# A list-scheduled attention and MLP kernel, planned with longer durations and longer hand-overs

## The chip, the cores and the metric
The kernel runs on one core of a Trainium2 chip. The metric is the device time of one execution in microseconds (us). The engines are called as in the profile: PE is TensorE (PEld its weight loads), DVE is VectorE, ACT is ScalarE, POOL is GpSimd, SP is SyncE, which issues the DMAs.

## The reference
Three stages follow one another. The attention keeps only scores near the row's maximum; the middle stage is a LayerNorm and a two-layer MLP with a residual; the last rotates by cosine and sine of a product, mixes tokens and channels, and adds.

```python
# attention: B=4, H=8, S=576, D=64
scores = q @ k.T / sqrt(64)
scores = where(scores >= max(scores) - tau, scores, -1e9)
x = softmax(scores) @ v                # -> [4, 576, 512]
# MLP
xn = (x - mean) / sqrt(var + 1e-6) * g
x = x + relu(xn @ w1) @ w2             # 512 -> 2048 -> 512
# mixing
theta = x @ w_theta
zr, zi = x * cos(theta), x * sin(theta)
y = w_tok_r @ zr + w_tok_i @ zi        # over the 576 tokens
u = x + y
out = u + relu(u @ w_ch)
```

## The kernel before
All work is written as a list of operations, and a planner orders it. `op` (class Plan, L288) records a function that emits one or a few instructions, the operations that it depends on, the buffers ("slots") that it takes and frees, a key, and for each engine that may run it a planned duration in ns (T for PE, V, A and G for DVE, ACT and POOL, Q for SP's DMAs). `run` (L319) plays the list several times in a planned time: `play` (L371) gives each engine its next ready operation, an operation with several possible engines goes to the one that would be done first by the plan, and after a dependency on another engine LAT ns pass before the user may start (`hop`, L366), after a DMA also DMA_LAT. `latest` (L345) works out from a played order how late each operation could start; these ranks, averaged over the plays, decide between ready operations on DVE, ACT, POOL and SP. PE takes the ready operation with the smallest key. Only the last play emits instructions, each engine's in the order of the plan. On the chip, instructions wait for semaphores; the planned time is not part of the program.

Planned durations are the numbers written at each `op` call, replaced by those in the table DUR where the operation's name and number stand there; DUR holds the mean durations of a profile.

Where the plan leaves PE idle for more than IDLE = 200 ns until the end of attention, `keep` (L620) writes filler matmuls (L626, 128x256, with a weight load each) into PE's order, as many as fill 0.7 of what is above 200 ns at 110 ns each:

```python
if e == "T" and self.idle and s - before > IDLE:
    self.idle(int((s - before - IDLE) * BUSY / 110.0), before)
```

Attention goes by batch b, tile t of 128 queries and head pair hp (`couple`, L1071): S_b_t_hp is the product of queries and keys (L1101). Batches 0 and 1 use f32 for it, 2 and 3 f16 halves in three products. There are two S buffers in PSUM (NS = 2), and a couple takes both. For each head (`unit`, L1197) DVE computes the row maximum ("top", L1208), ACT masks (L1224) and exponentiates (L1250), the weights are split into a high and a low f16 half (L465 to L478: copies on ACT, DVE or POOL, subtraction L478 on DVE or POOL), transposed by PE (tm, tl; L1179) or by DMA (L1271), and multiplied with v (pv_b_t_hp, L1116 to L1129). Buffers E (4) and P16 (4) hold scores and halves on the way. v is scaled first: pvs_b_hp (L990) sums a maximum, DVE turns it into a scale (L993), ACT applies it (va, L983 to L1008).

The batches are worked in pairs: 9 tiles of a pair form three groups; when a group's attention is done, `ln_group` (L1331) normalizes it, splits it and transposes it by DMA (L1405) into ringX, and `mlp1` (L873) runs the MLP for it: p_A, p_B (L883) and chA, c (L906); p1_A1_1_0 is the first product of the second pair's second group. Weights are read, scaled and split on the way (`cvt`, L634); pw_w2_8 (L781) sums a maximum for the scale of one part of w2, after ACT's L775. MLP matmuls and attention share PE from 106 us on; attention ends at about 417 us. Then come theta (L1883), z (`make_z`, L1941), y (`mix`, L2023, with L2074 and L2080) and o (`chan`, L2089, with L2105 and L2138).

## Time and profile before
| | us |
|---|---|
| median of 3 runs | 805.35 (805.19 to 805.42) |
| the profiled execution | 806.75 |
| its span | 805.0 |
| its mean granted clock | 0.998 |
| attention of batch 0 and the start of batch 1, without MLP matmuls | to 106.1 |
| attention beside the MLP, about | 106.1 to 417 |
| MLP and theta, z, y, o | the rest |

The span is what the profiler saw between the first and the last instruction; the profiled execution's own time has 1.75 us around it. Busy time is counted per engine, and engines run beside one another, so shares add up to more than 100%. A row of a timeline joins instructions of one kind that follow one another without a gap ("x8"). "idle before <-releaser" is how long the engine stood and what ended it. PEclk is the TensorE clock that was granted, as a share of full speed.

### The profile page before, as it was taken

The numbers are of one execution on the slowest core, as the hardware profiler recorded it, in microseconds if no ns is written. First come the engines' busy times: TensorE is split into PE (matmuls) and PEld (weight loads), VectorE is DVE, ScalarE is ACT, GpSimd is POOL, SyncE is SP. The second block draws the span as 40 slices with busy tenths as digits, with TensorE's granted clock in tenths as the row PEclk, the third lists the DMA queues.
The fourth block names the chain that finished last, engine by engine and source line by source line (L and its number), as shares of the span: only waits on it lengthen the run. The fifth ranks groups of instructions, "written<-read, shape, count | busy, mean of one in ns | idle before, by whom it ended". The sixth has DMA issues, their size and how long they took to land.

```text
span 805.0 us, 16588 instructions
## 1 busy us (share of the span) xinstructions
PE 789.7 (98%) x6189; PEld 516.8 (64%) x6189; DVE 650.4 (81%) x1310; ACT 510.0 (63%) x934; POOL 464.2 (58%) x551
## 2 busy tenths in 40 slices
PE   8999899999999999999999999999999999999998
PEld 6877766655566676666655555555545777567776
DVE  4999899999789897989867688777678795689843
ACT  5988899896797887898734243343476361474502
POOL 2767889878767676677436366635136370364711
PEclk9999999999999999999999999999999999999999
DMA  8565799987498998899894533663564005010011
GB/s 229 148 164 152 203 192 185 191 169 183 103 176 156 177 176 180 176 179 177 145 234 103 173 97 110 232 217 130 131 136 140 27 18 108 2 45 16 1 61 59
DMA packets 210833, 110.63 MB, mean 137 GB/s; under 512 B 173120, under 2 KB 191936, under 8 KB 210752
## 3 DMA queue, kind: packets, MB, share of 16 engines
q1 hardware_dynamic: 209936, 109.31, 57.8%
q8 instruction: 48, 0.79, 0.4%
q10 hardware_dynamic: 816, 0.26, 0.1%
q14 instruction: 33, 0.27, 0.1%
HBM read 52.50 MB, written 15.73 MB: 85 GB/s over the span
## 4 chain that ended last, share of the span: by engine, by line
PE 87%; DVE 6%; issue 2%; POOL 2%; ACT 1%; DMA 1%; SPq 0%; DVEq 0%; POOLq 0%
PE p_A L883 16%; PE chA L906 16%; PE y L2047 13%; PE S L1101 9%; PE p_B L883 6%; PE c L906 6%; PE th L1883 5%; PE o L2105 5%; PE pv L1129 4%; PE pv L1116 3%; PE pv L1124 3%; DVE ringE L1208 1%; PE tm L1179 1%; DMA raw_w<-in_w 1%; DVE w L706 1%
## 5 line engine op out<-in xcount | busy, mean ns | idle before, releaser
L883 PEld LDWEIGHTS <-w 128*128 128x128 f16 x1152 | 109.4, 98 | 79.7 <-issue 5.4
L906 PE MATMUL chA<-w,hbuf 128*128 128x512 f16 x648 | 149.9, 379 | 0.2 <-POOL w L478 0.2
L883 PE MATMUL p_A<-ringX,w 128*128 128x384 f16 x864 | 149.1, 326 | 0.0
L906 PEld LDWEIGHTS <-hbuf 128*128 128x128 f16 x864 | 80.8, 98 | 94.0 <-issue 5.8
L1208 DVE TENSOR_SCALAR_CACHE_REDUCE ringE<-S,ncoef 128x576 f32<-128x576 f32 x144 | 113.1, 809 | 14.5 <-PE S L1101 8.5
L478 POOL TENSOR_TENSOR ringP<-ringE,ringP 128x128 f16<-128x128 f32 (+2 forms) x109 | 102.0, 944 | 26.1 <-ACT ringP L465 17.4
L1224 ACT ACTIVATE ringE<-ringE,tiny 128x576 f32<-128x576 f32 x144 | 105.4, 768 | 9.3 <-POOL tiny L1216 4.9
L2047 PE MATMUL y<-tok,z 128*128 128x288 f16 x768 | 97.0, 286 | 0.0
L2047 PEld LDWEIGHTS <-z 128*128 128x128 f16 x768 | 75.1, 98 | 19.3
L1250 ACT ACTIVATE ringE<-ringE,ntaup 128x576 f32<-128x576 f32 x117 | 85.1, 764 | 0.0
L889 ACT ACTIVATE hbuf<-p_A 128x384 f16<-128x384 f32 x72 | 35.1, 488 | 49.8 <-PE p_A L883 46.8
L478 DVE TENSOR_TENSOR ringP<-ringE,ringP 128x512 f16<-128x512 f32 (+2 forms) x73 | 58.5, 813 | 2.4 <-ACT ringP L465 1.3
L1101 PE MATMUL S<-kf,qf 64*128 64x288 f32 (+1 forms) x288 | 53.4, 436 | 1.4 <-DVE ringE L1208 1.4
L469 POOL TENSOR_SCALAR ringP<-ringE 128x576 f16<-128x576 f32 x53 | 38.6, 731 | 23.7 <-ACT ringE L1250 19.6
L883 PE MATMUL p_B<-ringX,w 128*128 128x384 f16 x288 | 50.7, 326 | 0.0
L906 PE MATMUL c<-w,hbuf 128*128 128x512 f16 x216 | 50.6, 379 | 0.0
L1469 DVE SCALAR_TENSOR_TENSOR x<-chA,qs,x 128x512 f32<-128x512 f32 x54 | 40.2, 744 | 12.4 <-PE chA L906 12.1
L892 DVE SCALAR_TENSOR_TENSOR hbuf<-p_A,hbuf 128x384 f16<-128x384 f32 x72 | 39.7, 552 | 12.7 <-ACT hbuf L889 12.3
L2105 PE MATMUL o<-x1T,cw 128*128 128x288 f16 x360 | 44.9, 286 | 1.2 <-DVE x1T L2080 1.2
L473 ACT ACTIVATE x1T<-u,cs 128x576 f16<-128x576 f32 x15 | 11.6, 771 | 50.7 <-DVE u L2074 50.6
L1883 PE MATMUL th<-th,x1T 128*128 128x512 f16 x192 | 42.4, 379 | 0.0
L2105 PEld LDWEIGHTS <-cw 128*128 128x128 f16 x360 | 35.2, 98 | 10.4 <-issue 1.4
(267 smaller groups left out, 1578.0 us busy)
## 6 DMA issues: line engine op xcount, KB each, us to landing
raw_w<-in_w SPq DMA_DIRECT2D x20, 512.0 KB, 4.9
rawe<-in_w SPq DMA_DIRECT2D x12, 512.0 KB, 4.6
raw_tok<-in_wtok SPq DMA_DIRECT2D x12, 432.0 KB, 3.9
xscr<-x SPq DMA_DIRECT2D x18, 256.0 KB, 2.5
xl<-xscr SPq DMA_DIRECT2D x18, 256.0 KB, 4.9
out<-uo SPq DMA_DIRECT2D x15, 288.0 KB, 2.1
vraw<-in_v SPq DMA_DIRECT2D x13, 320.0 KB, 3.8
scr<-ringX SPq DMA_DIRECT2D x5, 768.0 KB, 4.6
```

Source lines behind the costliest of these rows:

```text
L478: e.tensor_tensor(out=out, in0=a, in1=b, op=ALU.subtract)
L883: T.matmul(st["ps"][:, :n], lhsT=ch.w1(a, c), rhs=xt()[:, c, bb, :n], start=(kk == 0), stop=(kk == 11))
L892: V.scalar_tensor_tensor(out=st["h"][:, 1, :n], in0=st["ps"][:, :n], scalar=0.0, in1=st["h"][:, 0, :n], op0=ALU.max, op1=ALU.subtract)
L906: T.matmul(ps, lhsT=h[:, a, t * 128:(t + 1) * 128], rhs=ch.w2(bb), start=(first and (a, bb) == M2[0]), stop=(stop and (a, bb) == M2[2]))
L1101: T.matmul(w["S"][:, n, 0:288], lhsT=qd.q[a][r, hp], rhs=d.k[c][r, n * 288:(n + 1) * 288], start=(k == 0), stop=(k == len(seq) - 1))
L1208: V.tensor_scalar(out=st["e"].rearrange("p (a k) -> p a k", a=2), in0=st["S"][:, :, 0:288], scalar1=ncoef, scalar2=None, op0=ALU.mult, op1 ...
L1224: A.activation(out=st["e"], in_=st["e"], func=AF.Prelu, bias=cp["thr"][:, j:j + 1], scale=-1.0, alpha=STEEP)
L1250: A.activation(out=e_of(ws), in_=e_of(ws), func=AF.Exp, bias=ntaup, scale=1.0)
L1469: V.scalar_tensor_tensor(out=x[p, t0 + t], in0=st["ch", t], scalar=chunks[i].quad.inv, in1=x[p, t0 + t], op0=ALU.mult, op1=ALU.add)
L1883: T.matmul(st["ps"], lhsT=src(a, c), rhs=w[:, c * 512:(c + 1) * 512], start=(kk == 0), stop=(kk == 11))
L2047: T.matmul(st["ps"][n][:, 0:288], lhsT=a, rhs=w[:, n * 288:(n + 1) * 288], start=(k == 0 and q == 0), stop=(k == 8 and q == 2))
L2105: T.matmul(st["ps"][n][:, 0:288], lhsT=w[:, cs], rhs=d["t"][a][:, kk, n * 288:(n + 1) * 288], start=(kk == 0 and q == 0), stop=(kk == 3 an ...
```

## The change
The table DUR and the lookup in `op` are taken out, so planned durations are the written ones: longer for most operations (a top is planned with 830 ns, not 764; a subtraction on DVE with 930, not 783; a step of S with 1230, not 1172), shorter for a few (a guard of the LayerNorm's scale 600, not 1274; chan.fin 457, not 675). LAT goes from 160 to 300 ns, DMA_LAT from 2500 to 2600. `run` no longer plays three times and emits the third; it plays 8 times, keeps the ranks with which the planned span was shortest, and emits a ninth play with those.

```diff
-LAT = 160.0
+LAT = 300.0
...
-DMA_LAT = 2500.0
+DMA_LAT = 2600.0
...
-PICK = 2
-DUR = {
-    "T": {
...
-        "couple.qk.go": {850: 896, 1000: 972, 1020: 990, 1230: 1172},
...
-        "unit.lo16.go": {930: 783},
...
-        "unit.top": {830: 764},
...
-        name = fn.__qualname__.replace("tile_kernel.<locals>.", "").replace("<locals>.", "")
-        engs = {e: DUR.get(e, {}).get(name, {}).get(round(ns), ns) for e, ns in engs.items()}
...
-    def run(self):
+    def run(self, passes=8):
...
-        rank = None
-        for k in range(PICK + 1):
+        best = rank = None
+        for k in range(passes + 1):
...
-            span = self.play(k == PICK)
+            if k == passes:
+                for o, r in zip(self.ops, best[1]):
+                    o.rank = r
+            span = self.play(k == passes)
+            if k == passes:
+                break
+            if best is None or span < best[0]:
+                best = span, [o.rank for o in self.ops]
             late = self.latest(span)
             rank = late if k == 0 else [0.5 * (a + b) for a, b in zip(rank, late)]
```

The program that comes out computes the same with the same instructions, but for three things: their order on each engine, the engine of some (of the 512-wide subtractions L478 118 stand on POOL, 100 before; 59 on DVE, 74 before), and the fillers: 92 instead of 44, 81 instead of 40 of them ahead of the first MLP matmul. Lines of the new kernel are 159 lower (S is L942, a top L1049, pv L957, a filler L467, the scale's L993 now L834).

Three places of the new order follow. In the names the last number is that of the buffer's allocation, which differs between the two.

The first is PE at the first change of the query tile in batch 0, from S_0_1_0 (the second tile's first head pair) to S_0_1_1. Before:

```order
L1101 MATMUL S_0_1_0_1_348<-kf_0_0_120,qf_0_1_228 128x288
L1116 MATMUL pv_0_0_2_360<-vraw_0_2_244,PT_0_0_2_0_329 128x65 x4
L1116 MATMUL pv_0_0_2_360<-vraw_0_2_244,ringP_88 128x65
L1116 MATMUL pv_0_0_2_360<-vraw_0_2_244,PT_0_0_2_1_354 128x65 x4
L1116 MATMUL pv_0_0_2_360<-vraw_0_2_244,ringP_88 128x65
L1101 MATMUL S_0_1_1_0_383<-kf_0_1_147,qf_0_1_228 128x288
```

and after (warm is a filler):

```order
L957 MATMUL pv_0_0_2_344<-vraw_0_2_225,ringP_88 128x65
L957 MATMUL pv_0_0_2_344<-vraw_0_2_225,PT_0_0_2_1_338 128x65 x4
L957 MATMUL pv_0_0_2_344<-vraw_0_2_225,ringP_88 128x65
L942 MATMUL S_0_1_0_0_367<-kf_0_0_120,qf_0_1_267 128x288
L942 MATMUL S_0_1_0_1_368<-kf_0_0_120,qf_0_1_267 128x288
L942 MATMUL S_0_1_0_0_367<-kf_0_0_120,qf_0_1_267 128x288
L942 MATMUL S_0_1_0_1_368<-kf_0_0_120,qf_0_1_267 128x288
L467 LDWEIGHTS one16_92
L467 MATMUL warm_24901_386<-one16_92 128x256
```

What moved: pv_0_0_2 stood between the two steps of S; now it stands ahead of the first, and behind that come 14 fillers (the last two rows are the first of them) and then S_0_1_1. S_0_2_0 and S_0_3_0 are followed by 16 fillers each.

The second is DVE at the start of batch 1, where the scale of v (pvs_1_0, L993 before, L834 after) is computed. Before:

```order
L1208 TENSOR_SCALAR ringE_87,tiny_89<-S_1_4_0_0_1142,ncoef_95 128x576
L706 SCALAR_TENSOR_TENSOR w1_4_1169<-raw_w1_4_1_700,qs_4_113,w1_4_1169 128x512
L467 COPY x_0_4_1194<-pv_0_4_0_1151 64x130
L706 SCALAR_TENSOR_TENSOR w1_4_1169<-raw_w1_4_0_623,qs_4_113,w1_4_1169 128x512
L706 SCALAR_TENSOR_TENSOR w1_4_1169<-raw_w1_4_2_793,qs_4_113,w1_4_1169 128x512
L993 TENSOR_SCALAR tiny_89<-pvs_1_0_1204 128x1
L706 SCALAR_TENSOR_TENSOR w1_4_1169<-raw_w1_4_3_857,qs_4_113,w1_4_1169 128x512
```

and after:

```order
L1049 TENSOR_SCALAR ringE_87,tiny_89<-S_1_4_0_0_1207,ncoef_95 128x576
L834 TENSOR_SCALAR tiny_89<-pvs_1_0_1217 128x1
L604 TENSOR_SCALAR tiny_89<-qs_4_113 128x4
L523 TENSOR_SCALAR a_w2_4_2_1172<-a_w2_4_2_1172 128x512
L1049 TENSOR_SCALAR ringE_87,tiny_89<-S_1_4_1_0_1219,ncoef_95 128x576
L608 SCALAR_TENSOR_TENSOR qs_4_113<-qs_4_113,tiny_89 128x4
```

The scale's operation stood behind three weight operations of 128x512 and a copy that follow the top of S_1_4_0; it now stands right behind that top.

The third is PE where the maximum of a weight part is summed (pw_w2_8), among the MLP's first products of the first pair (p1_A0_0_11). Before:

```order
L883 LDWEIGHTS w1_8_2606
L883 MATMUL p1_A0_0_11_2765<-ringX_80,w1_8_2606 128x384
L883 LDWEIGHTS w1_8_2606
L883 MATMUL p1_A0_0_11_2765<-ringX_80,w1_8_2606 128x384
L781 LDWEIGHTS one16_92
L781 MATMUL pw_w2_8_2773<-tiny_89,one16_92 128x1
L883 LDWEIGHTS w1_8_2606
L883 MATMUL p1_A0_0_11_2765<-ringX_80,w1_8_2606 128x384
```

and after:

```order
L942 MATMUL S_2_0_0_1_2821<-khi_2_0_2785,qhi_2_0_2648 128x288
L942 MATMUL S_2_0_0_0_2820<-khi_2_0_2785,qhi_2_0_2648 128x288
L942 MATMUL S_2_0_0_1_2821<-khi_2_0_2785,qhi_2_0_2648 128x288
L724 LDWEIGHTS w1_8_2603
L724 MATMUL p1_A0_0_11_2805<-ringX_80,w1_8_2603 128x384
L724 LDWEIGHTS w1_8_2603
L724 MATMUL p1_A0_0_11_2805<-ringX_80,w1_8_2603 128x384
L724 LDWEIGHTS w1_8_2603
L724 MATMUL p1_A0_0_11_2805<-ringX_80,w1_8_2603 128x384
L622 LDWEIGHTS one16_92
L622 MATMUL pw_w2_8_2844<-tiny_89,one16_92 128x1
```

The sum stands behind the third matmul of p1_A0_0_11 in both, but the whole step S_2_0_0 (12 matmuls, of which the last three are the first rows here) is now ahead of it.

## Rows read from the trace of the kernel before

**Rows 1.** The page's first part: busy time, share of the span, instructions.
```profile
PE 789.7 (98%) x6189; PEld 516.8 (64%) x6189; DVE 650.4 (81%) x1310; ACT 510.0 (63%) x934; POOL 464.2 (58%) x551
```

**Rows 2.** Busy time by stage: window, length, PE, PEld, DVE, ACT, POOL, clock, DMA share, GB/s.
```profile
6.00:106.10 100.10, 93.40 (x830) 75.88 (x829) 89.25 (x217) 85.41 (x168) 69.80 (x88) 0.98 0.68 180
106.10:404.00 297.90, 295.36 (x2754) 187.35 (x2752) 267.46 (x586) 249.04 (x440) 217.98 (x268) 1.00 0.88 170
```

**Rows 3.** PE's waits: for what, us in total, times, the longest.
```profile
PE pvs L990 <- ACT va L983: 2.9, 3, 1.9
PE pv L1124 <- DVE tiny L993: 1.8, 1, 1.8
PE pw_w L781 <- ACT tiny L775: 1.7, 1, 1.7
...
PE o L2105 <- DVE x1T L2080: 1.2, 1, 1.2
```

**Rows 4.** PE's timeline at 253 to 256 us: start, length, what.
```profile
253.29 0.78 PE L1101 MATMUL S<-khi,qlo 64*128 64x288 f32 x4
...
254.53 0.82 PE L906 MATMUL chA<-w,hbuf 128*128 128x512 f16 x3
255.19 0.60 PE L626 MATMUL warm<-one 128*128 128x256 bf16 x4
255.62 2.11 PE L883 MATMUL p_A<-ringX,w 128*128 128x384 f16 x12
```

**Rows 5.** PE's timeline, start of batch 0.
```profile
9.60 1.03 PE L626 MATMUL warm<-one 128*128 128x256 bf16 x8
...
13.69 1.97 PE L1101 MATMUL S<-kf,qf 64*128 64x288 f32 x8 [0.32 <-DVE ringE L1208]
```

**Rows 6.** DVE's timeline, the same stretch.
```profile
12.47 0.43 DVE L662 TENSOR_SCALAR a_w<-raw_w 128x512 uint32<-128x512 uint32 x1 [1.63 <-DMA raw_w<-in_w]
12.81 0.81 DVE L1208 TENSOR_SCALAR_CACHE_REDUCE ringE<-S,ncoef 128x576 f32<-128x576 f32 x1
```

**Rows 7.** PE's timeline at the first change of the query tile.
```profile
23.66 1.24 PE L1101 MATMUL S<-kf,qf 64*128 64x288 f32 x8
24.83 1.10 PE L1116 MATMUL pv<-vraw,PT 128*128 128x65 f32 x8
```

**Rows 8.** DVE's timeline, the second top of the same S.
```profile
25.68 0.81 DVE L1208 TENSOR_SCALAR_CACHE_REDUCE ringE<-S,ncoef 128x576 f32<-128x576 f32 x1
```

**Rows 9.** PE's timeline, behind the change to the third tile.
```profile
49.40 1.97 PE L1101 MATMUL S<-kf,qf 64*128 64x288 f32 x8 [0.70 <-DVE ringE L1208]
```

**Rows 10.** PE's timeline at 92 us; the window 90 to 100, columns as in rows 2.
```profile
92.41 1.69 PE L1124 MATMUL pv<-va,PT 128*128 128x65 f16 x28 [1.76 <-DVE tiny L993]
...
90.00:100.00 10.00, 8.24 (x74) 6.77 (x74) 7.24 (x17) 7.18 (x14) 8.55 (x13) 0.83 0.60 172
```

**Rows 11.** The LayerNorm of group (0,2): last pv, DMA transposes from 240 to 256 us.
```profile
222.78 1.01 PE L1124 MATMUL pv<-va,PT 128*128 128x65 f16 x28
...
L1405 SPq DMA_TRANSPOSE ringX<-xn x3: 1232/1296/1300, 244.0 to 250.4; - x3
...
DMA to landing us min/median/max: 3.0/3.3/3.3
```

**Rows 12.** PE's timeline ahead of the wait for x1T at 655 us.
```profile
648.13 7.02 PE L2105 MATMUL o<-x1T,cw 128*128 128x288 f16 x56
```

**Rows 13.** Groups by form: the 512-wide subtractions on POOL and on DVE.
```profile
L478 POOL TENSOR_TENSOR ringP<-ringE,ringP 128x512 f16<-128x512 f32 x59 | 71.8, 1220 | 14.2 <-ACT ringP L465 10.7 <-DVE ringP L467 0.9 <-DMA PT<-ringP 0.8
...
L478 DVE TENSOR_TENSOR ringP<-ringE,ringP 128x512 f16<-128x512 f32 x58 | 48.3, 841 | 2.3 <-ACT ringP L465 1.3 <-POOL ringP L469 0.8
```

**Rows 14.** DVE's timeline, then POOL's, around 649 us.
```profile
649.07 0.74 DVE L1970 SCALAR_TENSOR_TENSOR r<-xl,cs,r 128x512 f32<-128x512 f32 x1
649.72 1.77 DVE L1970 SCALAR_TENSOR_TENSOR co<-xl,cs,co 128x512 f32<-128x512 f32 x1
...
649.29 1.65 POOL L2074 TENSOR_TENSOR u<-u,x1T 128x576 f32<-128x576 f32 x1 [1.04 <-DVE u L2069]
```

158 lines of the change are left out of this document (removed).

## The prediction
> **What bounds the kernel now.** I read the page's first part, then the table of stages, then TensorE's waits, then timelines at the places that the order moves. TensorE is busy 98% of the span, the next engine, VectorE, 81% [rows 1]. The first two stages [rows 2], without the first six us: from 6.0 to 106.1 us (attention of batch 0 and the start of batch 1, before the first matmul of the MLP) TensorE is busy 93.40 of 100.1 us; from 106.1 to 404, beside the MLP, it misses 2.5 us of 297.9. So 6.7 of the 9.2 us that TensorE leaves open in the two lie in the first, and there its busy time holds fillers besides (the keep-warm matmuls of L626, 44 in all, 40 of them before the MLP). No order can win much more than the sum of these. The waits [rows 3] name the largest: on ScalarE's va (three, the longest 1.9 us), on VectorE's L993 (1.8), on ScalarE's L775 (1.7), on VectorE's x1T (1.2).
>
> The profiled execution took 806.75 us, a span of 805.0 and 1.75 around it; the median of the runs is 805.35, 1.40 lower. I sum differences against the profiled execution and carry them over to the median.
>
> **The change, part by part.** No arithmetic changes. What changes is the plan that decides order and engines, and how many fillers it writes: 44 before, 92 after. A filler costs 0.108 us: four of them begin at 255.19 and the next matmul at 255.62 [rows 4].
>
> *Start, a gain.* Before, 8 fillers stand behind pvs_0_3, from 9.60 on, and only then S_0_0_1; VectorE then starts on a weight (12.47, after 1.63 us of idling) ahead of that S's top, which so begins at 12.81, and the third S waits until 13.69 [rows 5, 6]. The new order has S_0_0_1 right behind pvs_0_3, and VectorE has both tops ahead of the weight. The 8 × 0.108 = 0.9 us of fillers go, and the top comes ahead of the weight (0.3 us); together that could be 1.2 us at the third S, or nothing if q and v land late. I take **−1.0** (0 to −1.2).
>
> *Tile boundaries of batch 0, a loss.* At S_0_1_0 the old order keeps pv_0_0_2 between this S and the next; the new one puts it ahead of S_0_1_0 and leaves only 14 fillers between S_0_1_0 and S_0_1_1 (16 at S_0_2_0 and at S_0_3_0). One step of S fills both S buffers, so the next must wait until both tops have read them: S starts at 23.66, the second top ends at 25.68 + 0.81 = 26.49, that is 2.83 us; the S itself occupies TensorE 24.83 − 23.66 = 1.17 [rows 7, 8]. The bubble is 1.66 us, with or without fillers in it. Before, pv filled it (from 24.83). New: 3 × 1.66 = 5.0, and 11 single fillers around these places, 1.2; together 6.2. Old: 22 fillers at the same boundaries, 2.4, and one wait of 0.70 at 49.40 [rows 9]: 3.1. The difference is **+3.1** (+1.0 if VectorE, which gets through its weights meanwhile, pays some back; +5.2 if each boundary adds a wait like that of 0.70).
>
> [...]
>
> *Before the MLP.* Seven fillers stand ahead of S_1_5_0 before, seven ahead of S_1_5_1 and four behind it after: 4 × 0.108 = **+0.4**.
>
> *pw_w2_8 (the 1.7 us wait of L781).* It moves behind S_2_0_0's twelve matmuls; twelve such take 254.53 − 253.29 = 1.24 us [rows 4]. That much of the wait is covered: **−1.2** (0 to −1.7).
>
> *LayerNorm of group (0,2).* The last matmul that it needs, pv_1_8_3, starts at 222.78, its last transposes are issued at 250.4 and land 3.3 us later, so the chain takes 30.9 us, and p_A starts at 255.62 [rows 4, 11]. The old order has 32.2 us of work between (fillers included), the new one 29.7, as I add up the matmuls between by their mean durations. So TensorE gets there some 1.2 us early and stands; it also lacks the four fillers and the idling (0.6) that the old one had. Net **+0.4** (0 to +1.5).
>
> *Batch 3's end.* Eleven fillers appear around S_3_8_3, ahead of p1_A1_1_0, where the old order has none: 11 × 0.108 = **+1.2** (0 if a wait stood there anyway; +2 if the LayerNorm of group (1,1) is later than planned).
>
> *Late hole.* At 656 us TensorE waits 1.16 us for x1T [rows 3]. The new order has six more o matmuls, 6 × 7.02 / 56 = 0.75 us by the mean of those before it [rows 12], ahead of the waiting one: **−0.7** (0 to −1.2). Of the three waits of L990 for va, two share 2.9 − 1.9 = 1.0 us [rows 3]; the later of them, 0.6 at 309.7 us, goes too, since its matmul now stands later: **−0.6** (0 to −0.6).
>
> *Engines.* POOL gets 18 more of the 512-wide subtractions that VectorE did (100 to 118); it takes 1220 ns for one, VectorE 841 [rows 13]. VectorE is shorter by 17 us over the whole kernel at its mean durations and POOL longer by 33. Both lie beside TensorE's work as long as E and P16 buffers come free in time; cover is POOL's share of 58%. At nothing here; its price without cover is a rival below.
>
> *Waits not in the old trace.* A new order makes new ones. The nearest rows are the waits that this order has, 1.2 to 1.9 us for a large one [rows 3]; I put **+0.5** for one, between −0.5 (small ones that go) and +3.
>
> Sum: −1.0 + 3.1 − 2.6 + 0.4 − 1.2 + 0.4 + 1.2 − 0.7 − 0.6 + 0.5 = −0.5. Profiled 806.3, on the median **804.9 us**: nothing that can be measured (0.2%, 1.6 us, is about what a measurement of this kernel tells from no change: 803.74 to 806.96). With all bounds at one end it would be 6.8 less or 10.1 more than that; as they hang on different waits, I take a third of each way, 802.5 to 808.5, for this case.
>
> **Rivals.**
> *Faster: batch 0 is not paced by TensorE.* If the MLP's start at 106 us hangs on the weights' preparation and on the tops rather than on matmuls, the boundary bubbles (+3.1) are paid by time that TensorE would have idled anyway, and no new wait appears (−0.5): −4.1, **801.2 us**. For it: VectorE is busy 89.25 of the 100.1 us and loses work; all fillers stand where TensorE was planned idle. Against it: from 23.66 us on, matmul follows matmul without a gap while tops and weights run on VectorE [rows 7].
>
> *Slower: POOL and VectorE block each other.* L1970 on VectorE takes 0.74 us at 649.07 and 1.77 at 649.72, when POOL has just begun L2074 [rows 14]: one us more for an operation beside POOL's. With 18 more two-operand subtractions on POOL, 18 × 1.0 us falls on VectorE's operations, tops among them, and 18 × (1.220 − 0.841) = 6.8 us on the chain mask, exp, hi, lo, transpose. It decides when the stretch's spare time is used up: VectorE has 10.9 us of it in the first stage. If a third of the 18 us delays tops that TensorE waits for, it is +6: **811 us**. [...] Against: VectorE's own list is shorter by 17 us, which pays for these 18.
>
> *Slower: the gaps are paid and the waits only move.* If L993's wait at 92 us, the one at 309.7 and that at 656 come back at other places because the operations that they wait for move with them, then −2.6 − 0.7 − 0.6 fall out: −0.5 + 3.9 = +3.4, **808.8 us**. For it: the plan takes a hand-over at 300 ns, but the waits of [rows 3] came from queues on VectorE and ScalarE that no plan foresaw. Against: in the new order L993 stands four operations earlier, and the waiting o and pv later.
>
> That the change does nothing is ruled out: the order differs at all these places.
>
> **Chances.** The forecast case 0.38 (0.08 of it below 803.74, 0.22 within 0.2%, 0.08 above 806.96). Faster rival 0.30. Contention 0.15. Gaps paid and waits moved 0.17, of which 0.03 within 0.2%. So faster 0.38, same 0.25, slower 0.37. The range 800.5 to 811.0 leaves out the faster rival's lower tail (about 0.1) and the upper end of the contention case (about 0.08).
>
> **What would show it.** In the changed kernel: S to S of 2.9 us at the three boundaries with fillers between; 92 fillers; no wait of 1.8 us on L993, and the granted clock from 90 to 100 us near 1.00; the first p_A between 105 and 107 us (103 in the faster rival); L781's wait below 0.6; 11 fillers shortly before p1_A1_1_0; o's wait below 0.6. The contention rival shows as tops (L1049 there) well over the 0.82 us of [rows 8] and as a larger S wait on it. I am wrong if the first p_A starts before 104 or after 109 us, or if one new wait of over 2 us appears after 106 us.

## The result, and the profile after

The new order is slower: median 812.83 us of 4 runs (811.01 to 815.68), the kernel before on the same chip 805.38 (805.19 to 806.27), ratio 1.008 [1.0061, 1.01]. The forecast was 804.9 in a range of 800.5 to 811.0; the result lies 1.8 us above the range. The profiled execution took 811.01 us, the shortest of the four, with a span of 809.2, which is 4.2 more than before. One execution among those below (rd_after's longest, 828.46 us at a mean granted clock of 0.949) fell into a slow state, and no ratio counts it.

The page's first part:

```profile
PE 796.4 (98%) x6237; PEld 521.9 (64%) x6237; DVE 644.4 (80%) x1288; ACT 509.2 (63%) x934; POOL 499.7 (62%) x576
```

TensorE's work is the same but for 48 more fillers (6237 against 6189 matmuls in [rows 1]). VectorE has 22 instructions fewer, POOL 25 more. The windows, columns as in [rows 2]; the first two are the stages shown there:

```profile
6.00:106.10 100.10, 97.92 (x883) 79.62 (x882) 91.47 (x226) 86.75 (x171) 73.89 (x91) 1.00 0.71 179
106.10:404.00 297.90, 292.37 (x2680) 184.41 (x2678) 258.04 (x542) 235.87 (x419) 223.70 (x268) 0.99 0.83 164
...
90.00:100.00 10.00, 10.00 (x128) 8.17 (x127) 10.00 (x30) 9.22 (x20) 9.49 (x14) 1.00 0.62 149
106.00:205.00 99.00, 93.47 (x874) 56.40 (x872) 95.35 (x190) 80.47 (x150) 86.53 (x96) 0.97 0.83 175
165.00:175.00 10.00, 9.57 (x71) 6.63 (x72) 8.93 (x19) 8.31 (x17) 6.71 (x11) 0.72 0.91 206
```

In the first stage TensorE is now busier (97.92 of 100.1 us against 93.40 in [rows 2]); in the second it misses 5.5 us of 297.9 instead of 2.5, at a clock of 0.99. The loss is beside the MLP, where the forecast had only small terms. For comparison, the same view of the kernel before, of 106 to 205 us and of ten us in it:

```profile
106.00:205.00 99.00, 97.27 (x912) 58.59 (x909) 96.11 (x208) 85.89 (x159) 85.24 (x98) 1.00 0.86 179
...
165.00:175.00 10.00, 10.00 (x105) 6.34 (x101) 9.31 (x23) 9.23 (x17) 8.20 (x11) 1.00 1.02 174
```

Before, TensorE stood nowhere between 102 and 193 us. VectorE was busy 96.11 of 99.0 us in this stretch and is now busy 95.35, but completes 18 instructions fewer, and TensorE 38. The waits of TensorE:

```profile
PE ptr L1252 <- ACT xn L1224: 3.0, 3, 1.3
PE p_A L724 <- DVE x L308: 2.1, 1, 2.1
PE tm L1020 <- ACT PT L1025: 1.2, 1, 1.2
PE S L942 <- DVE ringE L1049: 1.0, 3, 0.6
```

No wait of [rows 3] is left. In their place stand the waits for ScalarE's xn (the LayerNorm; L1252 are its transposes, ptr), one of 2.07 us for a copy on VectorE, and one of 1.2 for ScalarE's PT (at 57 us).

**Where the time went.** For each moment of a trace I take the time and subtract the nominal duration of all matmuls but fillers that TensorE has done by then (the same list in both kernels, each kind at one duration). What is left is lost time: waiting, fillers, a low clock. Its growth per stretch:

| stretch, us | lost before | lost after | difference | forecast |
|---|---|---|---|---|
| to 25: start | 6.4 | 4.3 | −2.1 | −1.0 |
| 25 to 80: tile boundaries | 8.2 | 10.8 | +2.6 | +3.1 |
| 80 to 100: the wait at 92 us, clock | 1.3 | −1.2 | −2.5 | −2.6 |
| 100 to 120: the MLP begins | 3.1 | 5.7 | +2.6 | +0.4 |
| 120 to 180: LayerNorm of group (0,1) | 1.6 | 8.2 | **+6.6** | 0 |
| 180 to 200: pw_w2_8 | 2.7 | 1.0 | −1.7 | −1.2 |
| 200 to 300: LayerNorm of (0,2) | 2.5 | 1.8 | −0.7 | +0.4 |
| 300 to 400: va | 4.1 | 3.0 | −1.1 | −0.6 |
| 400 to 500: batch 3's end | 0.1 | 1.6 | +1.5 | +1.2 |
| 500 to 700: x1T | 1.5 | 0.1 | −1.4 | −0.7 |
| 700 to the end | | | +0.4 | 0 |
| not placed | | | | +0.5 |
| sum | | | +4.2 | −0.5 |

(A loss below zero means that matmuls went a little faster than their nominal duration.) The rows hang on the durations chosen. With medians or means of the distance from one matmul's start to the next, 80 to 100 us comes out at −3.1 to −3.5, 100 to 120 at +3.1 to +3.6 and 120 to 180 at +6.7 to +7.3; the smaller rows, those between 300 and 500 us most, move by one us or more. The sum stays. Two rows miss by more than 2 us; each has its own place in the trace.

The first, at 111 us. TensorE's timeline, then VectorE's, then POOL's:

```profile
108.34 0.65 PE L724 MATMUL p_A<-ringX,w 128*128 128x384 f16 x3
111.06 2.60 PE L724 MATMUL p_A<-ringX,w 128*128 128x384 f16 x15 [2.07 <-DVE x L308]
...
108.38 2.20 DVE L319 TENSOR_TENSOR ringP<-ringE,ringP 128x64 f16<-128x64 f32 x2
...
110.71 0.51 DVE L308 COPY x<-pv 64x130 f32<-64x130 f32 x2
...
108.23 2.27 POOL L319 TENSOR_TENSOR ringP<-ringE,ringP 128x512 f16<-128x512 f32 x2
```

VectorE has two subtractions of 64 columns, which together take 2.20 us; the two copies of pv for which TensorE waits stand behind them. That is 1.14 us on the mean by the view of groups below, where six subtractions of twice the width take 0.36 us each. POOL's pair runs from 108.23 to 110.50, VectorE's from 108.38 to 110.58: the two lie over one another almost exactly, and each of VectorE's two ends 0.08 us behind one of POOL's.

The second, from 160 to 172 us. TensorE's timeline:

```profile
160.09 1.97 PE L942 MATMUL S<-kf,qf 64*128 64x288 f32 x8 [0.57 <-DVE ringE L1049]
163.39 0.85 PE L1252 MATMUL ptr<-ident,xn 128*128 128x128 f32 x4 [1.33 <-ACT xn L1224]
165.43 1.12 PE L1252 MATMUL ptr<-ident,xn 128*128 128x128 f32 x4 [1.19 <-ACT xn L1224]
...
166.48 2.29 PE L942 MATMUL S<-kf,qf 64*128 64x288 f32 x8
...
172.15 3.10 PE L724 MATMUL p_A<-ringX,w 128*128 128x384 f16 x18
```

Three waits (0.57, 1.33, 1.19) with two transposes of 0.85 and 1.12 us between them. The granted clock is 0.72 from 165 to 175 us by the window above, and 0.50 in the first half of it (165 to 170). Before, TensorE was busy 10.00 of 10.00 us there, at 1.00. What the transposes wait for, in the order VectorE, POOL, VectorE, ScalarE:

```profile
158.02 0.95 DVE L1197 TENSOR_SCALAR tiny<-tiny 128x3 f32<-128x3 f32 x1
...
159.05 0.97 POOL L1202 TENSOR_TENSOR tiny<-tiny,mhalf 128x3 f32<-128x3 f32 x1
...
161.99 0.15 DVE L1206 SCALAR_TENSOR_TENSOR tiny<-tiny 128x3 f32<-128x3 f32 x1
...
162.54 0.80 ACT L1224 ACTIVATE xn<-x,tiny 128x512 f32<-128x512 f32 x1
```

L1197, L1202, L1206 and L1224 are four links of one chain. L1206 is ready when POOL ends at 160.02 and starts at 161.99; a top and two weight operations (L516, L528) of VectorE's list are ahead of it. Before, the chain from the same first link to ScalarE's start took 153.37 − 150.05 = 3.3 us; now 162.54 − 158.02 = 4.5, and it begins 8 us later.

### The profile page after: what moved, and what is told of

Its sections match the earlier page's. It is cut to its first block, busy times and chain, and to the rows that moved or that the text cites. A ratio compares the mean times of both kernels' runs of the same rounds, so it can differ in the third digit from the quotient of the medians.

```text
span 809.2 us, 16681 instructions
## 1 busy us (share of the span) xinstructions
PE 796.4 (98%) x6237; PEld 521.9 (64%) x6237; DVE 644.4 (80%) x1288; ACT 509.2 (63%) x934; POOL 499.7 (62%) x576
## 4 chain that ended last, share of the span: by engine, by line
PE 88%; DVE 7%; POOL 2%; issue 1%; ACT 1%; DMA 1%; DVEq 0%; POOLq 0%; ACTq 0%
PE p_A L724 16%; PE chA L747 16%; PE y L1888 13%; PE S L942 9%; PE p_B L724 6%; PE c L747 6%; PE th L1724 5%; PE o L1946 4%; PE pv L970 4%; PE pv L957 3%; PE pv L965 2%; DVE ringE L1049 2%; PE tm L1020 1%; PE warm L467 1%; DVE w L547 1%
## 5 line engine op out<-in xcount | busy, mean ns | idle before, releaser
L747 PE MATMUL chA<-w,hbuf 128*128 128x512 f16 x648 | 148.1, 379 | 0.0
L319 POOL TENSOR_TENSOR ringP<-ringE,ringP 128x512 f16<-128x512 f32 (+2 forms) x120 | 119.4, 1008 | 12.9 <-ACT ringP L306 9.2
L1049 DVE TENSOR_SCALAR_CACHE_REDUCE ringE<-S,ncoef 128x576 f32<-128x576 f32 x144 | 112.4, 810 | 14.6 <-PE S L942 10.7
L310 POOL TENSOR_SCALAR ringP<-ringE 128x576 f16<-128x576 f32 x62 | 45.2, 733 | 34.0 <-ACT ringE L1091 33.7
L319 DVE TENSOR_TENSOR ringP<-ringE,ringP 128x512 f16<-128x512 f32 (+2 forms) x62 | 51.6, 843 | 7.3 <-ACT ringP L306 6.0
L942 PE MATMUL S<-kf,qf 64*128 64x288 f32 (+1 forms) x288 | 54.1, 440 | 1.0 <-DVE ringE L1049 1.0
L733 DVE SCALAR_TENSOR_TENSOR hbuf<-p_A,hbuf 128x384 f16<-128x384 f32 x72 | 39.6, 551 | 12.9 <-ACT hbuf L730 12.5
L970 PEld LDWEIGHTS <-PT 128*128 128x128 f16 (+1 forms) x720 | 36.9, 99 | 7.5 <-issue 3.5
L314 ACT ACTIVATE x1T<-u,cs 128x576 f16<-128x576 f32 x16 | 12.3, 770 | 45.8 <-DVE u L1915 41.1
```

Source lines behind the costliest of these rows:

```text
L310: G.tensor_scalar(out=out, in0=in_, scalar1=1.0, scalar2=0.0, op0=ALU.mult, op1=ALU.add)
L319: e.tensor_tensor(out=out, in0=a, in1=b, op=ALU.subtract)
L747: T.matmul(ps, lhsT=h[:, a, t * 128:(t + 1) * 128], rhs=ch.w2(bb), start=(first and (a, bb) == M2[0]), stop=(stop and (a, bb) == M2[2]))
L942: T.matmul(w["S"][:, n, 0:288], lhsT=qd.q[a][r, hp], rhs=d.k[c][r, n * 288:(n + 1) * 288], start=(k == 0), stop=(k == len(seq) - 1))
L970: T.matmul(out[:, j * 130:j * 130 + n], lhsT=pt[:, t, cs], rhs=va[:, :, t, js] if t < 5 else va[:, 0, t - 5, js], start=(t == 0), stop=(t ...
L1049: V.tensor_scalar(out=st["e"].rearrange("p (a k) -> p a k", a=2), in0=st["S"][:, :, 0:288], scalar1=ncoef, scalar2=None, op0=ALU.mult, op1 ...
```

## The experiments

All ratios are to the kernel before, on the same chip in the same batch (its median there lay between 806.3 and 807.6). In the diffs, `emit` is the planner's last play as a list; it is written out only after the moves. Three theories:

- **A.** The operations of the LayerNorm of group (0,1) come too late in VectorE's order; nothing else is short.
- **B.** POOL and VectorE hold each other up where both read SBUF.
- **C.** VectorE is full from 106 to 205 us and paces the stretch; what TensorE gains at one wait is given back at the next.

**again**: the changed kernel, unchanged, for the spread and a second trace.

> The changed kernel once more, unchanged, for a second trace and for its spread (811.0 to 815.7 us over four runs, where the kernel before stays within 1.1). Theory A (TensorE runs dry between 158 and 172 us, because the LayerNorm of group (0,1) comes late, and its clock falls there): 811 to 813 us, again a fall of the granted clock between 160 and 175 us, and where a run is longer than 811 it is by a second fall or a longer one. Theory B (the loss is spread: POOL and VectorE block each other): 811 to 813 us, no one place with more than 2 us lost.

Measured: 812.08 (810.73 to 813.1), 1.0065 [1.0039, 1.009]. Of its four executions, the two with a mean granted clock of 0.994 took 813.07 and 813.10, those with 0.996 and 0.997 took 811.08 and 810.73. So about 2 us of spread go with the clock. In this trace TensorE's timeline, then the windows:

```profile
111.57 4.11 PE L724 MATMUL p_A<-ringX,w 128*128 128x384 f16 x15 [2.07 <-DVE x L308]
```

```profile
112.00:114.00 2.00, 2.00 (x8) 0.88 (x6) 2.00 (x6) 0.00 (x0) 2.00 (x3) 0.50 1.09 200
114.00:116.00 2.00, 2.00 (x12) 1.03 (x12) 2.00 (x5) 0.77 (x2) 2.00 (x4) 0.83 0.12 26
```

The same wait of 2.07 us, and behind it the clock is 0.50 from 112 to 114 us and 0.83 on the mean of the next two. In the first trace it stayed at 1.00 behind the very same wait; those 15 matmuls end at 113.66 there. Its window:

```profile
112.00:114.00 2.00, 2.00 (x15) 1.15 (x14) 2.00 (x6) 0.79 (x2) 2.00 (x3) 1.00 0.91 169
```

**ln01_early**: theory A alone. Every operation of this LayerNorm goes to the place, in the order of emission, right behind the last operation that it depends on.

```diff
...
+        for r in [r for r in emit if r[0] in self.early]:
+            i = emit.index(r)
+            need = set(map(id, list(r[0].deps) + list(r[0].prev)))
+            j = max((k for k in range(i) if id(emit[k][0]) in need), default=-1) + 1
+            emit.insert(j, emit.pop(i))
...
```

> The changed kernel with one thing moved: on VectorE, POOL and ScalarE the eleven operations of the LayerNorm of group (0,1) (statistics, r1, r2, r3, norm) stand as early as their inputs allow; order of everything else and all of TensorE's order as it was. Theory A: the two waits of the transposes ptr (1.3 and 1.2 us) and the fall of the clock there (3.7 us lost) go, 5 to 6 us less, about 805.5 us. Theory B: at most 1 us less, 810 to 812.

Measured: 814.12, 1.0093 [1.0071, 1.0116]: no gain. Among TensorE's waits one large row is new, and the ptr row is smaller:

```profile
PE chA L760 <- DVE hbuf L746: 2.7, 1, 2.7
...
PE ptr L1267 <- ACT xn L1239: 1.4, 2, 0.9
```

VectorE now stands at operations whose input POOL has not finished (1.27 us up to 148.87, 0.98 up to 154.26), and what is behind them (hbuf) makes TensorE wait 2.7 us.

**ln01_mid**: nine of these operations moved less far, so that none should stand in front of its engine.

```diff
+MOVES = [(836, 808), (839, 836), (853, 839), (854, 853), (859, 854), (866, 825), (879, 831), (884, 863), (895, 884)]
...
+        for what, after in MOVES:
+            r, k = emit[what], emit[after]
+            self.todo = getattr(self, "todo", []) + [(r, k)]
+        for r, k in self.todo:
+            emit.remove(r)
+            emit.insert(emit.index(k) + 1, r)
```

> The changed kernel with the LayerNorm of group (0,1) moved ahead, but less far than in ln01_early: the statistics and r1 right behind the last scaling of x on VectorE (150 us), r2 on POOL behind the subtraction that follows, r3 four operations later, the first two norms on ScalarE ahead of the threshold and the masks at 160 us. No operation should stand waiting for another engine. If the late LayerNorm is a cause of its own: the waits of ptr (1.3 and 1.2 us) and the clock's fall behind them go, 3 to 5 us less, 807 to 809. If VectorE's load decides (theory C): the waits go, but tops, masks and weights come later by as much, TensorE waits at the next S or weight, 811 to 813.

Measured: 813.35, 1.0069 [1.005, 1.0087], just above the 811 to 813 that C expected. Among the waits, two new rows and ptr:

```profile
PE pw_w L639 <- ACT tiny L633: 2.5, 1, 2.5
...
PE chA L764 <- DVE hbuf L750: 1.5, 1, 1.5
PE ptr L1269 <- ACT xn L1241: 1.4, 2, 1.0
```

The ptr row falls from 3.0 to 1.4 us, and 4.0 us of other waits appear. In both runs the waits that A names shrink and the time does not fall, so A falls.

**a_evict**: the wait at 111 us alone; VectorE's two copies go ahead of the two subtractions (the code of ln01_mid, with other numbers).

```diff
+MOVES = [(569, 576), (566, 576)]
```

> The changed kernel with one move: at 109 us the two copies of pv (L308) ahead of the two 64-wide subtractions on VectorE (2.2 us, beside one of POOL's), so that TensorE does not wait 2.1 us for them at 111. If waits of TensorE add up: -2 to -4 (with the clock's fall behind the wait), 808 to 810. Theory C: the wait goes, VectorE has the same work, by 200 us it is given back, 811 to 813.

Measured: 811.33, 1.006 [1.0043, 1.0077], an interval that overlaps that of the changed kernel. The wait of 2.07 us is gone; the 18 matmuls that it had cut in two (3 and 15) run as one row:

```profile
108.93 3.32 PE L741 MATMUL p_A<-ringX,w 128*128 128x384 f16 x18
```

By 140 us the lost time is back where it was. This is C's value.

**ptr_fill**: ten fillers ahead of each of the first two transposes of group (0,1), to keep the clock up through the waits.

```diff
+                if nm == "0_1":
+                    for _ in range((10, 10, 0)[t - 0]):
+                        T.matmul(st["pt", t][:, 0:2, :].rearrange("p c k -> p (c k)"), lhsT=one16[:, 0:128], rhs=one16, start=True, stop=True)
```

> The changed kernel with ten keep-warm matmuls (1.08 us) ahead of each of the first two transposes of group (0,1), where TensorE stands 1.3 and 1.2 us; the waits stay. If the clock falls because TensorE stands there: granted clock 1.00 from 160 to 175 us, waits as they were, 3.0 to 3.7 us less, about 807.5. If the clock falls for another reason, or the fillers come too late: no change, 811 to 813.

Measured: 811.17, 1.0055 [1.0037, 1.0074]. TensorE's timeline, then a window:

```profile
162.62 1.27 PE L1259 MATMUL ptr<-one 128*128 128x256 bf16 x10
...
169.44 1.97 PE L948 MATMUL S<-kf,qf 64*128 64x288 f32 x8
171.35 1.96 PE L730 MATMUL p_A<-ringX,w 128*128 128x384 f16 x11
```

```profile
165.00:170.00 5.00, 4.59 (x55) 3.28 (x52) 5.00 (x11) 4.64 (x11) 3.94 (x6) 1.00 0.79 192
```

With fillers in the two waits the clock stayed at 1.00 where it had been 0.50 (165 to 170). (The two traces at 111 us show that the length of one wait alone doesn't decide: behind the same 2.07 us it was 1.00 in the first and 0.50 in again.) And yet the next p_A began at 171.35 instead of 172.15: the clock kept up was worth 0.8 us in these traces. Its S that begins at 169.44 takes 1.97 us at a clock of 1.00, where an unhindered one takes 1.24 (at 166.65 us), so the matmuls don't set the pace there; the tops that free its two buffers do, I take it.

**no_bound_fill**: the 57 fillers at and around the tile boundaries of batch 0 left out.

```diff
+        if 20000.0 < now < 90000.0:
+            return
```

> The changed kernel without the 57 keep-warm matmuls between 20 and 90 us of the plan (tile boundaries of batch 0); order otherwise as it was. The prediction's reading, that the bubble behind S_0_1_0, S_0_2_0 and S_0_3_0 is set by the tops and that the 46 fillers in it are free: at most the 11 single ones go (1.2 us), 810 to 812 us, unless the clock falls in the bubbles (then up to 3 us longer). If the fillers themselves are the price: 57 x 0.108 = 6 us less, 805.

Measured: 813.03, 1.008 [1.0054, 1.0106]; the lost time at 80 us is 15.1 us with them and without. The bubble is the wait for the tops, and fillers in it cost nothing, as the forecast had it. The single ones around these places, for which it had counted 1.2 us, cost nothing that this run shows either.

**mem_after, mem_before, rd_after**: theory B. In the first two (the changed kernel, the kernel before) POOL's subtractions of the low halves of batch 1 are replaced by two memsets each, which write the same place twice and read nothing; the low halves of batch 1 are then zero. In rd_after POOL subtracts a constant from itself: it again reads two SBUF operands of the same width, but waits for no data, and the low halves are zero too.

```diff
+                if e is G and nm[0] == "1":
+                    for _ in range(2):
+                        G.memset(p_of(ws)[:, :, 640:1152], 0.0)
+                    return
... (rd_after:)
+                if e is G and nm[0] == "1":
+                    for w in ws:
+                        out = ringP[:, w["s16"].i, 640:1152].rearrange("p (a k) -> p a k", a=4)
+                        src = ident.unsqueeze(1).to_broadcast([128, 4, 128])
+                        sub(e, out, src, src)
+                    return
... (and the like for the last 64 of the 576 columns)
```

> The changed kernel, where POOL's subtractions for batch 1 (the low halves of its softmax weights) are left out: in their place POOL writes zeros twice over the same half, so it is busy about as long but reads nothing. Order and waits are otherwise the same. Theory B (VectorE is full from 106 to 205 us, and its operations are stretched by POOL's reads: over the 10th percentile of their own form they lose 23.8 us there, 16.6 in the kernel before): the stretch of VectorE's operations there falls to 10 to 15 us, the transposes ptr of group (0,1) come 4 to 6 us earlier, 805 to 807 us. Theory A (only the order of the LayerNorm's operations counts): 810 to 812.

> The same in the kernel before: POOL's subtractions of batch 1 left out for writes of zeros. Theory B: VectorE's stretch there falls from 16.6 us to about 10, but TensorE loses only 7 us between 106 and 205 us and part of that is for other reasons: 803 to 804.5 us, so less than the changed kernel gains. Theory A: 805 to 806.

> The control to mem_after: the changed kernel, POOL's subtractions of batch 1 again left out, and again replaced by work on the same halves that waits for none of the data, but now a subtraction of two SBUF operands (the identity from itself), so it reads. If it was the reads that held VectorE up (theory B): VectorE's stretch from 106 to 205 us is again above 20 us and the time 809 to 813. If mem_after gained because the replacement waits for nothing and frees its buffers earlier: 804 to 806, as mem_after (804.9).

Measured: mem_after 804.88, 0.9981 [0.9972, 0.999]; mem_before 804.65, 0.9978 [0.9964, 0.9991]; rd_after 808.87, 1.0029 [1.0018, 1.0041]. Without these subtractions the two orders are equal within their intervals. Groups by form between 106 and 205 us, VectorE's 512-wide subtraction, then POOL's; before, after, mem_after, rd_after:

```profile
L478 DVE TENSOR_TENSOR ringP<-ringE,ringP 128x512 f16<-128x512 f32 x15 | 12.2, 831 | 0.0
...
L478 POOL TENSOR_TENSOR ringP<-ringE,ringP 128x512 f16<-128x512 f32 x19 | 23.9, 1261 | 0.7
```

```profile
L1049 DVE TENSOR_SCALAR_CACHE_REDUCE ringE<-S,ncoef 128x576 f32<-128x576 f32 x32 | 24.9, 809 | 2.5 <-POOL ringP L319 1.4 <-PE S L942 1.1
L319 DVE TENSOR_TENSOR ringP<-ringE,ringP 128x512 f16<-128x512 f32 x14 | 15.0, 1075 | 0.3 <-POOL ringP L310 0.3
...
L319 DVE TENSOR_TENSOR ringP<-ringE,ringP 128x64 f16<-128x64 f32 x2 | 2.2, 1140 | 0.0
L319 DVE TENSOR_TENSOR ringP<-ringE,ringP 128x128 f16<-128x128 f32 x6 | 2.2, 360 | 0.0
...
L319 POOL TENSOR_TENSOR ringP<-ringE,ringP 128x512 f16<-128x512 f32 x19 | 24.3, 1283 | 0.2
```

```profile
L1049 DVE TENSOR_SCALAR_CACHE_REDUCE ringE<-S,ncoef 128x576 f32<-128x576 f32 x34 | 26.4, 809 | 2.3 <-PE S L942 2.2
L319 DVE TENSOR_TENSOR ringP<-ringE,ringP 128x512 f16<-128x512 f32 x14 | 10.7, 763 | 0.6 <-POOL ringP L310 0.6
...
L1103 POOL MEMSET ringP<- 128x512 f16 x40 | 21.6, 542 | 1.3
```

```profile
L319 DVE TENSOR_TENSOR ringP<-ringE,ringP 128x512 f16<-128x512 f32 x14 | 14.7, 1051 | 0.1
```

VectorE's subtraction reads two SBUF operands. Its mean is 1075 ns in the changed kernel, 1051 beside POOL operations that read and wait for nothing, 763 beside POOL operations that only write. The top, which reads one operand from PSUM, keeps its 809 ns in after and in mem_after. Over all of VectorE's operations of the stretch (each against the tenth percentile of its own form) the lengthening is 16.6 us before, 23.8 after, 23.0 in rd_after, 18.1 in mem_after. In time: rd_after less mem_after, 808.87 − 804.88 = 4.0 us, hangs on POOL's reads (up to a part for POOL itself, which is busy 87.46 us of the stretch in rd_after and 83.71 in mem_after). The changed kernel less rd_after hangs on the rest, what the subtractions wait for and the buffers that they hold, which I did not tell apart: by ratios 1.0073 (the mean of the two batches) − 1.0029, some 3.5 us. In the kernel before, the whole of it is worth 0.22%, 1.8 us; the part of the reads in that was not tried. So the reads explain between 4.0 − 1.8 = 2.2 and 4.0 us of the difference between the two orders.

The number of subtractions is not it: POOL has 19 of the 512-wide ones here in both kernels. Nor is it how much of VectorE's 512-wide subtractions lies beside POOL's operations: nearly all of it in both traces (11.7 of 12.5 us before, 14.1 of 15.0 after, added up one by one). But before, one of 15 took over 1.0 us, and after, seven of 14 (1.11 to 1.65). Why the new order stretches more of them is not shown.

**dv_after, dv_before**: VectorE's own 512-wide subtractions of batch 1 replaced by a memset of 64 columns, in the changed kernel and in the one before; these low halves are then left out. By the groups above these are 14 of VectorE's operations in the stretch and 15.0 us, and the memsets take 0.085 us each; POOL's work stays.

```diff
+                if e is V and nm[0] == "1":
+                    V.memset(p_of(ws)[:, :, 640:704], 0.0)
+                    return
```

> The changed kernel with VectorE's own 512-wide subtractions of batch 1 left out (the low halves of those softmax weights; 15 of some 1.0 us, in their place a write of 64 columns): the same order and the same waits, some 14 us less for VectorE between 100 and 210 us. Theory C (VectorE's load paces this stretch of the changed kernel): the waits of p_A at 111 us and of ptr at 163 us shrink or go, 803 to 806 us. If the loss lies in TensorE's own order and fillers: 810 to 812.

> The same in the kernel before (15 of some 0.83 us, 11 us less for VectorE). Theory C: TensorE stands little there already (some 2 us at 193 us and 1 to 2 us spread), so 803 to 805 us: the two kernels come within 2 us of one another, as in mem_after and mem_before.

Measured: dv_after 809.16, 1.003 [1.0014, 1.0046]; dv_before 805.26, 0.9984 [0.9975, 0.9994]. Some 14 us less on VectorE bring 3.4 us (1.0073 − 1.003 of 806), where C expected 803 to 806 us, and the two kernels stay 3.9 us apart, where it expected 2. So C fails as it was put: VectorE's load alone does not pace the stretch. What is left of it is that gains are given back, in a stretch where POOL and ScalarE too are busy 86 and 87% of the time (85.24 and 85.89 of 99.0 us before); that their fullness is the reason is my reading. TensorE's wait for xn stays at 3.0 us and that for the copy at 2.1, at the same places.

**p_lat, p_dur, q_pick2, q_lat160**: the three parts of the change apart. p_lat is the kernel before with LAT 300 and DMA_LAT 2600; p_dur the kernel before with DUR empty; q_pick2 the changed kernel with three plays and no choice; q_lat160 the changed kernel with the old LAT and DMA_LAT. (The choice of the best play alone, with the old durations and hand-overs, gives the program of before, instruction by instruction.)

```diff
-LAT = 160.0
+LAT = 300.0
...
-        best = rank = None
-        for k in range(passes + 1):
+        rank = None
+        for k in range(2 + 1):
```

> The kernel before with the longer hand-overs alone (LAT 300, DMA_LAT 2600); measured durations and three plays as before. If the longer hand-over is what makes the new order slow: 810 to 813 us, with bubbles and fillers at the tile boundaries of batch 0 and a late LayerNorm of group (0,1). If the written durations are: 805 to 807.

> The kernel before with the written durations alone (table DUR empty); hand-overs of 160 ns and three plays as before. If the written durations are what makes the new order slow: 809 to 813 us. If the longer hand-over is: 805 to 807. The plan's choice of the best of 8 plays is not run alone, since with both other parts as before it writes the same order as the kernel before.

> The changed kernel (written durations, LAT 300) with the plays of the kernel before: three, the third is emitted, no choice of the best. It plans 128 fillers, the changed kernel 92. If the choice by the planned span picks orders that run well: slower than the changed kernel, 813 to 820. If the planned span says little about the chip: within 3 us of 812 on either side.

> The changed kernel with hand-overs of 160 ns (LAT 160, DMA_LAT 2500): written durations and the best of 8 plays. The run p_dur (same, but three plays) took 813.3, q_pick2 (LAT 300, three plays) 819.2, the changed kernel 812.5. If the choice among 8 plays is worth some 6 us in general: 806 to 809. If every newly planned order falls where it falls: 810 to 816, with its losses at other places than in the changed kernel.

| planned durations | LAT | plays | median, us | ratio |
|---|---|---|---|---|
| DUR (before) | 160 | third | 805.4 | 1 |
| DUR (p_lat) | 300 | third | 813.4 | 1.0089 [1.0064, 1.0113] |
| as written (p_dur) | 160 | third | 813.3 | 1.0089 [1.0073, 1.0104] |
| as written (q_pick2) | 300 | third | 819.2 | 1.0153 [1.0136, 1.0171] |
| as written (the change) | 300 | best of 8 | 812.8 | 1.008 [1.0061, 1.01] |
| as written (q_lat160) | 160 | best of 8 | 815.3 | 1.0102 [1.0077, 1.0126] |

Each part alone costs as much as the whole, and not at the same place: lost time up to 100 us is 15.9 us before, 13.9 after, 19.6 in p_lat, 13.6 in p_dur; from 100 to 200 it is 7.4, 14.9, 12.3 and 14.4 (by other nominal durations the differences move by about one us). The choice among 8 plays wins 6.4 us at LAT 300 and nothing at LAT 160. I read this as scatter: all five new orders lie between 1.008 and 1.0153, and none of them improves on the one that had been kept. Five orders are few. If all six were draws of one kind, the old one would be the best of them once in six times, so a reason that favours it is not ruled out; none was found beyond the stretch named above.

**h_two**: the two gains that the forecast was surest of, put into the kernel before and nothing else: L993 ahead of the three weight operations (92 us), and L2080 ahead of L1970 (x1T at 656 us), by MOVES as above.

```diff
+MOVES = [(456, 462), (452, 462), (445, 462), (3477, 3471)]
```

> The kernel before with two moves on VectorE: the scale of pvs_1_0 (L993) ahead of the three weight operations, as in the changed kernel, and at 651 us the low half of x1T (L2080) ahead of the multiplication L1970 that stood before it. The prediction's reading (TensorE paces, so waits on it add up): -1.8 to -3.5 for the first and -1.2 for the second, 801 to 802.5 by the median of 805.4. Theory C (VectorE is full from 106 to 205 us and paces that stretch, so what TensorE gains ahead of it is given back; after 404 us TensorE paces): the wait at 92 us and the low clock go, but by 200 us nothing of it is left; only the 1.2 of the second stay, 804 to 805.5.

Measured: 805.03 (11 runs), 0.9983 [0.9973, 0.9993]: faster by 1.4 us, the best of all that compute the whole. The window 90 to 100, and TensorE's timeline from 95 to 106 and at 650 us (rows with a wait, and o):

```profile
90.00:100.00 10.00, 8.08 (x98) 6.47 (x98) 8.95 (x18) 7.95 (x17) 8.33 (x13) 1.00 0.61 164
```

```profile
96.62 1.24 PE L1118 MATMUL S<-kf,qf 128*128 128x288 f32 x4 [0.89 <-DVE ringE L1225]
...
99.25 1.07 PE L1141 MATMUL pv<-va,PT 128*64 128x65 f16 x28 [0.51 <-DMA PT<-ringP]
...
101.65 0.66 PE L1428 MATMUL ptr<-ident,xn 128*128 128x128 f32 x4 [1.33 <-DVE xn L1403]
...
647.69 11.92 PE L2122 MATMUL o<-x1T,cw 128*128 128x288 f16 x96
```

Both waits are gone, the clock stays at 1.00, and o runs through. At 95 us the lost time is 3.0 us less than before (13.2 against 16.2; 2.1 to 3.1 less by other nominal durations). At 105 us it is 0.2 less (18.0 against 18.2): a top, a DMA and xn make TensorE wait 2.7 us between, where the kernel before waited 0.6 for xn alone. At 660 us it is 1.8 less. So the gain at 92 us was given back in ten us, and what is left is mostly that of the late hole, behind attention. The place lies ahead of the stretch from 106 us on, with VectorE busy 8.95 of 10.00 us: not only the fullest stretch gives back.

## Why the prediction was wrong

**What held.** The bubbles at the boundaries: S to S takes 26.31 − 23.50 = 2.81 us with 14 fillers between, +2.6 against +3.1. TensorE's timeline at the first of them:

```profile
23.50 1.24 PE L942 MATMUL S<-kf,qf 64*128 64x288 f32 x8
24.68 1.70 PE L467 MATMUL warm<-one 128*128 128x256 bf16 x14
26.31 1.53 PE L942 MATMUL S<-kf,qf 64*128 64x288 f32 x8
```

The wait at 92 us: the −2.6 of the sum is a value that no run shows. The runs show that the wait of 1.76 us is gone, that the clock from 90 to 100 us is 1.00 where it was 0.83 [rows 10] (0.50 from 93 to 95 us before), and a difference of −2.5 in the ledger (−3.1 to −3.5 by other nominal durations). By [rows 10] alone I estimate wait and clock together at 1.76 + (1 − 0.83) × 10 = 3.5 us, so −2.5 lies beside −2.6 in part by chance. The eleven fillers at batch 3's end: +1.5 against +1.2. pw_w2_8: −1.7 against −1.2, its whole wait went. x1T: −1.4 against −0.7; o runs without a gap, so the six matmuls ahead of it covered all of the wait. The start: −2.1 against −1.0. S_0_0_2 begins at 11.93 instead of 13.69 [rows 5]. Of these 1.8 us, 0.8 come from the fillers and the top, for which I had 1.0; the other 1.0 us is pvs_0_3 itself, which now starts at 8.59 and before at 9.57, behind the longest wait for va of [rows 3]. I had not seen that the new order serves it sooner. First p_A: 104.62, 0.4 us ahead of the named window of 105 to 107.

**What did not.** The LayerNorm of group (0,2): −0.7 against +0.4 (0 to +1.5); TensorE has no wait between 205 and 404 us in the new trace. And the sign of being wrong that I had named came: one new wait of over 2 us after 106 us, the 2.07 us at 111.

**The step that failed** is "Waits not in the old trace", +0.5 with an upper end of +3, together with "Engines … At nothing here". Between 100 and 180 us the measured difference is +9.2 (9.8 to 10.9 by the other durations), of which +0.4 are fillers. All other rows together came out at 4.2 − 8.8 = −4.6, where the forecast had −1.0 for them. I had bounded the term by the size of one wait of [rows 3]. The new order of the stretch from 106 to 205 us makes several waits, some with a low clock behind them (0.50 from 165 to 170 us), and repairing one place alone brought little or nothing (ln01_early, ln01_mid, a_evict, ptr_fill: 1.0093, 1.0069, 1.006 and 1.0055, the changed kernel 1.0065 and 1.008).

The cover that I named for "at nothing", POOL's share of 58%, is an average over the whole span. In this stretch VectorE was busy 97% of the time before, POOL 86%, ScalarE 87% (96.11, 85.24 and 85.89 of 99.0 us). There was little cover to begin with: [rows 2] already had POOL at 73% and VectorE at 90% from 106 to 404 us. I also had VectorE's list shorter by 17 us and POOL's longer by 33, by mean durations. POOL's busy time grew by 35.5 us (464.2 to 499.7), but VectorE's fell only by 6.0 (650.4 to 644.4): its operations became longer, which a sum of mean durations leaves out.

**The nearest rival** was contention (811 us), right about the mechanism and wrong about its place: I charged it to the 18 more subtractions on POOL, but 19 stand in this stretch in both orders, and its 811 us came from a third of 18 us, so that it lies near the result is luck; I had it delay tops, and tops kept 0.81 us [rows 8]. It struck VectorE's subtraction of two SBUF operands (1051 ns beside POOL's reads, 763 beside its writes), and by mem_after and rd_after some 4 us of the new order's time hang on it, of which between 2.2 and 4.0 us are new.

**From the profile to the median.** I carried the sum over as it stood: the median of before lay 1.40 us below its profiled execution. The changed kernel's median lies 1.8 above its own. Of the miss of 812.8 − 804.9 = 7.9 us, 4.7 stand in the ledger (+4.2 against −0.5), and 3.2 come from this. The new order has waits behind which the clock falls in some executions and not in others (at 112 to 114 us 0.50 in again, 1.00 in the first trace). One sum of the prediction is off: its upper bounds lie 10.8 us above the forecast, not 10.1; no argument hangs on it.

## What to carry to other kernels

Before costing a reordering, look at the windows of each stage for every engine, not only for the one that bounds. Here, with VectorE busy 97%, ScalarE 87% and POOL 86% of a stretch, what was gained at one wait was given back within tens of us, and the new order cost more than the waits that could be named beforehand. Make a ledger of lost time by stretch for both traces; it says which terms held, here to about one us. And an order that a planner calls shorter is not shorter on the chip for that: the five new ones here were 0.8 to 1.5% longer than the old. Measure several and keep the best, or move single operations where an engine has room, as h_two did at 656 us.

## What the runs showed of the hardware

The same wait of 2.07 us, with the same instructions around it, was followed by a granted clock of 1.00 in one execution (after, 112 to 114 us) and of 0.50 in another (again). A subtraction of 64 columns took 1.14 us beside POOL's subtraction of 512, three times the mean of those twice as wide (0.36 us); the two timelines at 108 us lie as if each of VectorE's pair ended only with its partner on POOL, 0.08 us behind it. In a_evict, where this pair starts 1.0 us behind POOL's and not 0.15, it took 1.34 us and again ended 0.08 us behind POOL's. And a clock that was kept up where it had been 0.50 for five us gave back 0.8 us (ptr_fill).
